# Retention and token/channel mixer on one core: states of three pairs of batch 0 as running sums in PSUM

## The chip, the cores and the metric

The kernel runs on one core of a Trainium2 chip. The core has five engines that run side by side and wait for each other by semaphores: TensorE (PE in the profile; its weight loads are PEld), VectorE (DVE), ScalarE (ACT), GpSimd (POOL) and SyncE (SP). SBUF is the working memory, PSUM (eight banks of 512 f32 columns on 128 partitions) takes what PE writes. The metric is the device time of one execution in microseconds (us), the median of several runs; lower is better.

## The reference

For 4 batches and 8 heads, 768 steps and 64 columns a head, a state decays by a factor `gamma` of its head and takes up an outer product at each step; the query reads it. The result is the input of a mixer over tokens, then one over channels, each with a residual.

```python
gamma = 1.0 - 2.0 ** (-5.0 - np.arange(H))
scale = 1.0 / np.sqrt(D)
for t in range(S):
    state = gamma * state + einsum('bhd,bhe->bhde', k[:, :, t], v[:, :, t])
    y[:, :, t] = scale * einsum('bhd,bhde->bhe', q[:, :, t], state)
x = y.transpose(0, 2, 1, 3).reshape(B, S, H * D)
h = relu(x.transpose(0, 2, 1) @ w_tok1) @ w_tok2
u = x + h.transpose(0, 2, 1)
out = u + relu(u @ w_ch1) @ w_ch2
```

## The kernel before

**Fronts.** For each batch and each pair of heads (4 x 4 fronts) the 768 steps are six chunks of 128. k is scaled by a power of gamma that runs within a chunk (`decayed`, L337; one instruction a head, L343 on ACT or L345 on DVE). k and q are turned by PE (L376, L381), k's turned form is copied out of PSUM (`evkT`, L395), q's is multiplied by a curve of powers on its way out (`qev`, L390). The curves are made once, by exponentials on ACT (L247), of step numbers that GpSimd writes (L235). Within a chunk the scores k x q (`sc`, L457) are masked (`am`, L469) and multiplied with v (`av`, L483). Across chunks, five products k x v (`st`, L410) leave one 64x64 state of each chunk and head in PSUM; U, the running state, is formed on DVE: a copy of the first (L419), then four steps U(c) = g128 U(c-1) + state(c) (L425), where g128 is gamma to the 128th. Two scalings by g128 (`rs`, L435 or L437) put it into block-diagonal tiles `cross` (three of them, tag `rz`), and five products with q add what came from earlier chunks (`y2`, L494). The sum is copied out as x (`xev`, L503). The token mixer follows: `t1` (L520) with w_tok1, relu to h (L529, L531), `t2` (L541) with w_tok2 onto the same bank, u copied out twice (`uev` in f16, `Xev` in f32, both L503), and u turned to `uT` (`tru`, L579, L585; in later batches by DMA).

**Backs.** The channel mixer widens 512 to 1536 columns (`w8`, L617, plain for batch 0's first blocks; P1 to P7, L689, seven products in place of eight) and narrows again (N1 to N7, L787). The seven-product forms need sums: of weights (`asum`, L902; `wsum`, L889), of u (`ts`, L661) and of h (`sm`, L765). X takes up the result (L801) and is stored (L744). The first widening products need uT of pairs 0 to 2 and the first part of w_ch1; wsum needs the whole of w_ch2 (`wc2`, three loads).

**What sets the order.** The program has no scheduler at run time and none that plans at build time: `ORDERED` lists its 1244 operations in the order in which they are issued, `WAYS` says for those with a choice whether ACT or DVE does them, `PLACES` which of the buffers or banks each tile gets, and `FILLS` how many products with zeros PE does ahead of an operation (L921, only in the start-up). Each engine works through its own share in that order, waiting where it must. Loads are issued by GpSimd (L303, L299, and L283 for weights), all on one queue in that order; SP issues the first three (q of pair 0, k of pair 0, q of pair 1), the turnings by DMA and the stores.

Of the kernel before, what the change touches and what calls it, by code (L numbers as in the profile page):

```python
# [10 lines left out]
FP = mybir.dt.float32  # L11
# [5 lines left out]
OPT = dict(wide7=(1, 2, 3), mix=4, turned=(), whole=0, held='qkQ', lead='v00', am=1, turns='twt twt twt twt twt twt twx twx xxx xxx xxx xxx xxx xxx xxx xxx')  # L17
# [10 lines left out]
class Op:  # L28
# [30 lines left out]
    "cW7dd6cPdc707ed71a7fcS726Xdpd86Ydf1c6ZdqcT7gd97hdtcU1jdgdddadr71diduds7idjdedw7jdDdx7kdv8Idn7ldhdEdy",
    "dBdodRdk8LdF7mdzdCdl8adSdAdHdG7ndm7pdTdI8MdV8bdU8N7QdWdK7U7rdYdL7ScD7odXdZ7T1f6v7qdJe07se3dP7Re4e1dM",  # L60
    "dQ7t8d8Je2dN7ueLe98edO7y8fea7ve57A7I8ge69j8OePeM8c7w7ze7eb7JeQe8cE7xed7K8h7B7LeReNee8ief7Mec8K7Neh7O",
    "7PeT8j73eg8Pei8k7W9R7VeUem8Q1e9g8l8R7X7YeSeV7Zen80eOej9h8SeW81bYeqeXek828Tcjes8o8mer83eY8qeZ848p8586",
    "8sf287888neu899O8reAf0ev8Uf39i8WeB9Pey8X9kf18t8V8u8v8w8Zewf4ezci8Y9leC8xf68yexeEel8z9091eF9m8Af79UeD",
    "929Vet938B959W94eH9X969Y9n9S8E8C9ZfaeI8D97f8fb8Ffo8Gfc9o988HeGfefpfgf9ff99fd9pfq9Q9afh9bfsfr9q9c9rfi",
    "ft9T9u9efjfm9wfvfnfk9yfwfQflfC9dg49vfD9ffu9xfAfRfGfxf5fSfBeofHfEg5fya0fTfJ9s9t9zfUfFfzfIfKg6fWfVfLfO",
    "g7fXfPgifY9AfMgjfZ9C9Bg8fNg09D9Egkgmg9g1g2a19Fgng3glgb9GgpeJa2gqgc9Ha69Ka4gugga5gvgoghgAa3gagrhggda7",
    "gshchhge9Jgthi9Ihd9Ma8a9heaahkab9Lachm9NhlgVhngfhohfhqhjhpgRadgThtgWgSgXaehugZgYgwafh0aigUgBh1hrgxgC",
    "gyh3agajgEh2alh4hsgGgzgFh5hvgDakgIh6gHh8gJahgKhxgNh9h7hBgLhahPhyhCi3hbhzhQiheKhFgOhRgMhGhThHhAgPhUhI",
    "hShwhVhJhWiihDhXhKhNilhYhOi1hEhLivgQhMhZi4ijimiJiki2i7ioi0iKinipi5i8i9iqiaitibiNi6iriciLepisifiwidiM",
    "iOizixieiQigiPiAiBiyiCiRjsiDiSiuiViEiHiWiTiIjtj1jJjNjLiFjKjOjTiUjRjoj2jUjPjqjSjXiGjQjVjpjYjyjWjMjwjz",  # L70
    "k0jrjxjZjCiXjAk2iYjujBiZj5k1jDk3j7jEj6jFjvjHj9jGj8j3jIjaj0jbjej4jhjijcjljgjjjdjkjmjfjn00",
)
WAYS = (
    "0000000000000000000000000000000000000000000000000000000000000000000000000000000000000000000010100010",
    "0000000000000000000100100100100000000000000000000000010010000100000000000000000000000000101000001100",
    "0000000000000000000010010000000011000000000001000000000000000000000100000000000000000000000000000000",
    "0001000000000000000000000000100100000100000100000000000000010000000010000010010000000000000000000010",
    "0100100010010000000000000001000001000011000000000010000000000000000000000001100100001000000000000000",
    "0000101101000000000000000000000000000100000010000000000000000000000010000000000000000001000000000100",
    "0000010010001000000010000000000000101000100000000000000000000000000000000000000000000000000000000000",  # L80
    "0000000000000000000000000000000000000000000000000000000000000000000000000000000000011000000000000000",
    "0000000000010000100000000100000000001000000000000000000000000000000000000000000000000000000010000000",
    "0000000000000010000000001000000000100000000000000000000000010000000000000100000001000000000000000000",
    "0000000001000101001000000000000000000000000100000010000000000000110000000000000000000110000000000000",
    "0000000010000000000000001000000010101000000000000010000000001000001001000000000000000000000001110000",
    "00000000000000000000011000000000000010000000",
)
PLACES = (
    "0001101001001021202234506030121131421313054264500356220104250710325040030321403507221110221217311640",
    "7122050662333121702310100571420233504020010216435017025132103012031503016107205231445736501161021745",  # L90
    "2412024211223330200034611012103134061252201112611020741120473534602017533011032201211150212012001765",
    "0324021501640175637303300610710212141127430001221037561124103750302600047316272342045710003511307412",
    "1201601151101233211062701120603012275234476051002751230011220113463173130024571125210303417106430072",
    "2140435244564572011314360702301120230061024017130516413210541102504173601120131",
)
FILLS = (
    (93, 6), (95, 8), (105, 2), (110, 3), (141, 2), (166, 1), (176, 2),
# [18 lines left out]
def kernel(  # L116
# [117 lines left out]
    def emit():  # L234
        nc.gpsimd.iota(tile_of(SINCE, [P, HC, P], FP), pattern=[[0, HC], [1, P]], base=-MID, channel_multiplier=0,  # L235
                       allow_small_or_imprecise_dtypes=True)
    since_op = prep("since", "POOL", 450, emit, takes=[SINCE])
    gq_ops = []
    for p in range(NP):
        def emit(p=p):  # L240
            for j in range(2):
# [3 lines left out]
        def emit(p=p):  # L245
            gq = tile_of(GQ, [P, NP, SH], FP) if GQ.tile is None else GQ.tile
            nc.scalar.activation(gq[:, p], SINCE.tile.rearrange("p i t -> p (i t)"), AF.Exp, bias=lnsc, scale=lnh[:, p:p + 1])  # L247
# [705 lines left out]
```

## Time and profile before

| what | us |
|---|---|
| median of three runs | 186.19 (186.18 to 186.61) |
| the profiled execution | 186.44 |
| its span on the core | 184.7 |
| first to last product of PE | 1.2 to 181.1 |
| TensorE clock granted, mean | 0.999 |

A page of the profile gives each engine's busy time, then the span in 40 slices with the busy share of each in tenths, the DMA queues, and the chain of work that ended last, followed back from the last instruction. A row of the timeline has start, duration, engine, line, operation, tiles written and read with their shapes, and a count where equal ones are merged (the duration then runs from the first start to the last end). Durations of neighbours overlap, so one instruction's cost to its engine is the distance of two starts. A row of the chain has start, the part of time put down to it, engine, tile and line.

These rows are the costliest groups of the start-up on ACT and DVE (0 to 33 us): busy time and mean ns of one, then idle time ahead of them.

```profile
L469 DVE TENSOR_TENSOR am<-psum,mask 128x384 f16<-128x384 f32 x17 | 8.9, 548 | 0.7 <-PE psum L457 0.6
L390 DVE TENSOR_TENSOR qT<-psum,X 128x768 f16<-128x768 f16 x5 | 4.8, 953 | 1.5 <-PE psum L381 1.2 <-PE psum L376 0.2
L425 DVE SCALAR_TENSOR_TENSOR U<-U,gp,psum 128x64 f32<-128x64 f32 x16 | 4.1, 273 | 0.6 <-ACT U L419 0.5
```
```profile
L435 ACT ACTIVATE cross<-U,gp 64x320 f16<-64x320 f32 x8 | 4.5, 556 | 0.1
L343 ACT ACTIVATE k<-k,gk 128x384 f16<-128x384 f16 x5 | 3.0, 613 | 0.7 <-DMA k<-in_k_dram 0.7
```

The eight scalings into `cross` and the sixteen U steps are those of the four pairs of batch 0.

### The profile page before, as it was taken

The numbers are of one execution on the slowest core, as the hardware profiler recorded it, in microseconds if no ns is written. First come the engines' busy times: TensorE is split into PE (matmuls) and PEld (weight loads), VectorE is DVE, ScalarE is ACT, GpSimd is POOL, SyncE is SP. The second block draws the span as 40 slices with busy tenths as digits, with TensorE's granted clock in tenths as the row PEclk, the third lists the DMA queues.
The fourth block names the chain that finished last, engine by engine and source line by source line (L and its number), as shares of the span: only waits on it lengthen the run. The fifth ranks groups of instructions, "written<-read, shape, count | busy, mean of one in ns | idle before, by whom it ended". The sixth has DMA issues, their size and how long they took to land.

```text
span 184.7 us, 5233 instructions
## 1 busy us (share of the span) xinstructions
PE 175.5 (95%) x2054; PEld 133.7 (72%) x2054; DVE 168.7 (91%) x424; ACT 131.5 (71%) x302; POOL 52.2 (28%) x61
## 2 busy tenths in 40 slices
PE   7877989999999999999999999999999999999992
PEld 2445878666688988786568988966678986667881
DVE  5599889999999999999999999989888989889993
ACT  3659989869889997899999778679835324855120
POOL 7985656485282201099020200000000000000000
PEclk9999999999999999999999999999999999999999
DMA  6999999999999999799999895446011034410054
GB/s 158 197 163 184 176 194 207 185 182 194 178 156 158 149 147 131 162 129 139 156 149 227 163 198 132 115 91 166 32 57 31 15 99 171 175 57 0 4 187 155
DMA packets 93993, 25.71 MB, mean 139 GB/s; under 512 B 83600, under 2 KB 91152, under 8 KB 93968
## 3 DMA queue, kind: packets, MB, share of 16 engines
q0 software_dynamic: 67184, 12.78, 85.0%
q1 hardware_dynamic: 25056, 9.83, 25.7%
q10 hardware_dynamic: 1728, 2.75, 4.3%
q8 instruction: 16, 0.26, 0.6%
q14 instruction: 9, 0.07, 0.1%
HBM read 26.74 MB, written 6.29 MB: 179 GB/s over the span
## 4 chain that ended last, share of the span: by engine, by line
PE 71%; DVE 19%; ACT 4%; DMA 2%; issue 2%; DVEq 0%; ACTq 0%
PE psum L689 24%; PE psum L787 23%; PE psum L617 6%; DVE am L469 5%; PE psum L541 4%; PE psum L520 3%; DVE X L801 3%; PE psum L457 3%; DVE U L425 2%; DMA hs<-in_q_dram 2%; DVE hs L765 2%; PE psum L483 2%; PE psum L381 1%; PE psum L376 1%; DVE k L345 1%
## 5 line engine op out<-in xcount | busy, mean ns | idle before, releaser
L642 ACT COPY us<-psum 128x384 f32<-128x384 f32 (+1 forms) x52 | 22.2, 433 | 20.1 <-PE psum L787 13.9
L469 DVE TENSOR_TENSOR am<-psum,mask 128x384 f16<-128x384 f32 x64 | 32.6, 548 | 1.3 <-PE psum L457 1.0
L787 PEld LDWEIGHTS <-hs 128*128 128x128 f16 x282 | 26.6, 98 | 3.7 <-issue 0.4
L303 POOL DMA_DIRECT2D v<-in_v_dram x16 | 16.6, 1036 | 36.9 <-PE psum L494 11.3
L689 PE MATMUL psum<-hs,late 128*128 128x384 f16 x120 | 26.5, 326 | 0.2 <-ACT h L529 0.2
L637 ACT ACTIVATE h<-psum 128x384 f16<-128x384 f32 x47 | 21.8, 492 | 4.4 <-PE psum L617 2.3
L710 DVE CUSTOM_DVE_ANT_0 h<-psum,us 128x384 f16<-128x384 f32 x40 | 21.3, 549 | 1.9 <-ACT us L642 1.3
L787 PEld LDWEIGHTS <-h 128*128 128x128 f16 x216 | 20.6, 98 | 3.1
L689 PEld LDWEIGHTS <-late 128*128 128x128 f16 x160 | 14.9, 98 | 9.3 <-issue 0.4
L801 DVE TENSOR_TENSOR X<-X,psum 128x256 f32<-128x256 f32 (+1 forms) x49 | 19.4, 407 | 1.4 <-PE psum L787 0.7
L787 PE MATMUL psum<-wsum,hs 128*128 128x256 f16 x144 | 19.3, 273 | 0.0
L787 PE MATMUL psum<-wc,h 128*128 128x256 f16 x144 | 19.3, 273 | 0.0
L787 PE MATMUL psum<-wc,hs 128*128 128x256 f16 x138 | 18.7, 273 | 0.0
L303 POOL DMA_DIRECT2D k<-in_k_dram x15 | 15.4, 1030 | 8.6 <-ACT k L343 2.8
L689 PE MATMUL psum<-uT,wc 128*128 128x384 f16 x80 | 17.6, 326 | 0.0
L642 ACT COPY psum<-psum 128x384 f32<-128x384 f32 (+1 forms) x30 | 12.8, 432 | 6.6 <-PE psum L787 3.4
L425 DVE SCALAR_TENSOR_TENSOR U<-U,gp,psum 128x64 f32<-128x64 f32 x64 | 16.3, 273 | 0.9 <-ACT U L419 0.5
L435 ACT ACTIVATE cross<-U,gp 64x320 f16<-64x320 f32 x27 | 15.0, 557 | 1.6 <-DVE U L425 1.1
L689 PEld LDWEIGHTS <-wc 128*128 128x128 f16 x120 | 11.1, 98 | 6.2 <-issue 0.2
L541 PE MATMUL psum<-h,wt 128*128 128x128 f16 x192 | 14.7, 219 | 0.0
L503 ACT CAST x<-psum 128x384 f16<-128x384 f32 x28 | 13.2, 481 | 1.7 <-PE psum L494 0.9
L520 PE MATMUL psum<-x,wt 128*128 128x128 f16 x192 | 13.3, 219 | 0.8 <-ACT X L503 0.6
(90 smaller groups left out, 341.6 us busy)
## 6 DMA issues: line engine op xcount, KB each, us to landing
v<-in_v_dram POOLq DMA_DIRECT2D x16, 192.0 KB, 8.4
out_dram<-X SPq DMA_DIRECT2D x12, 256.0 KB, 2.5
k<-in_k_dram POOLq DMA_DIRECT2D x15, 192.0 KB, 8.3
q<-in_q_dram POOLq DMA_DIRECT2D x14, 192.0 KB, 9.9
wc<-in_moe_w_ch_dram POOLq DMA_DIRECT2D x5, 512.0 KB, 11.5
out_dram<-X ACTq DMA_DIRECT2D x10, 256.0 KB, 2.8
hs<-in_q_dram SPq DMA_DIRECT2D x2, 384.0 KB, 5.0
wc<-in_moe_w_ch_dram POOLq DMA_DIRECT2D x2, 256.0 KB, 9.6
```

The source lines that it names most:

```text
L303: (nc.sync if hard else nc.gpsimd).dma_start(out=tile_of(s, [P, 2, NC, D], FP if hard else F16), in_=src.rearrange("h (c p) d -> p (h c) d ...
L425: nc.vector.scalar_tensor_tensor(out=u[:, c], in0=u[:, c - 1], scalar=gp[:, p:p + 1], in1=chunk(c), op0=ALU.mult, op1=ALU.add)
L435: nc.scalar.activation(r, u, AF.Copy, scale=g)
L469: nc.vector.tensor_tensor(am, SC[g].tile[:, :SH].rearrange("p (i t) -> p i t", t=P), mask.to_broadcast([P, HC, P]), ALU.mult)
L520: nc.tensor.matmul(acc[:, jt * P:(jt + 1) * P], wt1[:, i, jt * P:(jt + 1) * P], X16.tile[:, i].rearrange("p h d -> p (h d)"), start=(i == ...
L541: nc.tensor.matmul(Y[j].tile[:, 2 * i * D:2 * (i + 1) * D], wt2[:, jt, t], H1.tile[:, jt], start=False, stop=(jt == NJ - 1), skip_group_ch ...
L637: nc.scalar.activation(out, src, AF.Relu)
L642: (nc.scalar.copy if e == "ACT" else nc.vector.tensor_copy)(out, src)
L689: nc.tensor.matmul(acc[:, :SH], left(ct), r[:, ct], start=first and ct == 0, stop=ct == C2 - 1, skip_group_check=True)
L710: nc.vector._custom_dve(TENSOR_ADD_SAT, out=h(m, sh), in0=R.tile[:, :SH], in1=KS.tile[:, j], s0=BIG, s1=0.0)
L787: nc.tensor.matmul(acc[:, lo], l[:, j], r[:, j], start=first and j == 0, stop=j == K2 - 1, skip_group_check=True)
L801: nc.vector.tensor_tensor(dst(), dst(), b_(), ALU.add)
```

## The change

For pairs 1, 2 and 3 of batch 0 (`long`), powers of gamma no longer run over one chunk of 128 tokens but over three, 384 tokens, so that chunk states with one scale can be summed by PE in PSUM. k takes its factor from a table `gk2` with three columns (chunk of the half), so each head's scaling is three instructions of 128 columns, each over two chunks. q takes its factor from a second set of curves (three more exponentials on ACT, over a second iota on GpSimd). PE then writes five sums: of chunks 0; 0 and 1; 3; 3 and 4; 0, 1 and 2 (18 products in place of 10). Four evacuations put them into `cross` straight from PSUM: per head a plain copy of the four near sums (`rsn`) and a scaling of the far one by gamma to the 384th (`rsf`). The U copy, the four U steps and the two `rs` of these pairs fall away. The second half's chunks 4 and 5 read two sums each, the near one and the far one, so `y2` has seven products instead of five. Pair 0 of batch 0 and the other batches work as before.

```diff
+        PARTS = ((0,), (0, 1), (3,), (3, 4), (0, 1, 2)) if long else tuple((c,) for c in range(NC - 1))
         def emit():
             st = tile_of(ST, [P, 512], FP)
-            for c in range(NC - 1):
-                for j in range(2):
-                    nc.tensor.matmul(st[rows_of(j), c * D:(c + 1) * D], K.tile[:, c, j], V.tile[:, j, c],
-                                     start=(c == 0), stop=True, skip_group_check=True)
+            for n_, cs in enumerate(PARTS):
+                for c in cs:
+                    for j in range(2):
+                        nc.tensor.matmul(st[rows_of(j), n_ * D:(n_ + 1) * D], K.tile[:, c, j], V.tile[:, j, c],
+                                         start=(n_ == 0), stop=(c == cs[-1]), skip_group_check=True)
...
+        for j, far_ in ((j, x) for j in range(2 if long else 0) for x in range(2)):
+            def emit(e, j=j, far_=far_):
+                cs = slice(NC - 2, NC - 1) if far_ else slice(0, NC - 2)
+                r = opened(RS, None, F16)[rows_of(j), cs, j]
+                u = ST.tile[rows_of(j), cs.start * D:cs.stop * D].rearrange("p (c d) -> p c d", d=D)
+                if e == "ACT" and far_:
+                    nc.scalar.activation(r, u, AF.Copy, scale=g384[rows_of(j), p:p + 1])
+                elif e == "ACT":
+                    nc.scalar.copy(r, u)
...
+            for j in range(2 if long else 0):
+                def emit(e, j=j):
+                    t, h = opened(dst, [P, NC, 2, D], F16)[:, :, j], 2 * p + j
+                    for i in range(HC):
+                        if e == "ACT":
+                            nc.scalar.activation(t[:, i::HC], src.tile[:, j, i::HC], AF.Copy, scale=gk2[:, h, i:i + 1])
...
-            cs = range(max(1, hf * HC), (hf + 1) * HC)
+            cs = [(c, c - 1) for c in range(max(1, hf * HC), (hf + 1) * HC)]
+            if long:
+                cs = [(3, 4), (4, 4), (4, 2), (5, 4), (5, 3)] if hf else [(1, 0), (2, 1)]
...
+            gq2_ops[p] = prep("gq2", "ACT", 620, emit, [since2_op, lnh_op, lgm_op], [], [SINCE, GQ])
...
 FILLS = (
-    (93, 6), (95, 8), (105, 2), (110, 3), (141, 2), (166, 1), (176, 2),
+    (102, 2), (104, 11), (114, 3), (119, 3), (138, 1), (147, 3), (174, 1), (179, 1),
 )
```

The tables `ORDERED`, `WAYS`, `PLACES` and `FILLS` are new throughout: with operations gone and added, the order of all of them, the engine of those with a choice and the banks were chosen afresh. New line numbers stand for old ones thus: L381 and L383 the short decays, L390 and L392 the old ones, L254 and L261 the curves, L443 evkT, L461 st, L488 rs, L499 rsf, L501 rsn, L526 sc, L538 am, L574 the copies of x, u and X, L591 t1, L688 the plain widening, L960 wsum.

Three places of the new order. First ACT, from the scaling of k of pair 1 to the first x, before; `cross` is the block-diagonal state, U the running state, `X_133` the curves, `x` the copies of x.

```order
L343 ACTIVATE k_225<-k_117,gk 128x6x64
L247 ACTIVATE X_133<-us_114,lnsc,lnh 128x384
L395 COPY kT_259<-psum 128x768
L419 COPY U_265<-psum 128x64
L343 ACTIVATE k_283<-k_137,gk 128x6x64 x2
L435 ACTIVATE cross_79<-U_218,gp 64x5x64 x2
L395 COPY kT_325<-psum 128x768
L435 ACTIVATE cross_80<-U_265,gp 64x5x64
L343 ACTIVATE k_337<-k_162,gk 128x6x64
L503 CAST x_359<-psum 128x384
```

The same place of the change, in part: from the turned k of pair 1 to the scaling of k of pair 3.

```order
L443 COPY kT_287<-psum 128x768
L381 ACTIVATE k_291<-k_142,gk_82 128x2x64 x3
L501 CAST cross_79<-psum 64x4x64
L488 ACTIVATE cross_80<-U_233,gp 64x5x64
L499 ACTIVATE cross_79<-psum,g_84 64x64
L443 COPY kT_342<-psum 128x768
L499 ACTIVATE cross_79<-psum,g_84 64x64
L501 CAST cross_79<-psum 64x4x64
L488 ACTIVATE cross_80<-U_233,gp 64x5x64
L501 CAST cross_81<-psum 64x4x64
L499 ACTIVATE cross_81<-psum,g_84 64x64 x2
L381 ACTIVATE k_392<-k_184,gk_82 128x2x64 x6
```

Twelve short decays (three ahead of the first row shown, nine in it) now stand on ACT ahead of the first x, with six evacuations from PSUM; two of the four x copies ahead of t1 are on DVE.

Second DVE, from the second masking of pair 0 to the first of pair 1, before.

```order
L469 TENSOR_TENSOR am_220<-psum,mask 128x384
L425 SCALAR_TENSOR_TENSOR U_218<-U_218,gp,psum 128x64
L469 TENSOR_TENSOR am_223<-psum,mask 128x384
L345 TENSOR_SCALAR k_225<-k_117,gk 128x6x64
L425 SCALAR_TENSOR_TENSOR U_218<-U_218,gp,psum 128x64
L390 TENSOR_TENSOR qT_240<-psum,X_133 128x768
L469 TENSOR_TENSOR am_261<-psum,mask 128x384
```

And in the change, from the third masking of pair 0 on.

```order
L538 TENSOR_TENSOR am_235<-psum,mask 128x384
L383 TENSOR_SCALAR k_237<-k_124,gk_82 128x2x64 x3
L479 SCALAR_TENSOR_TENSOR U_233<-U_233,gp,psum 128x64
L438 TENSOR_TENSOR qT_256<-psum,X_126 128x768
L479 SCALAR_TENSOR_TENSOR U_233<-U_233,gp,psum 128x64 x2
L538 TENSOR_TENSOR am_289<-psum,mask 128x384
L383 TENSOR_SCALAR k_291<-k_142,gk_82 128x2x64 x3
```

Only pair 0 keeps its U steps; the steps of pairs 1 to 3, which stood between the maskings further on, are gone.

Third the loads on GpSimd's queue, ahead of the token mixer's second weights (`wt_83`), before.

```order
L303 DMA k_137<-in_k_dram 128x12x64
L299 DMA q_156<-in_q_dram 128x2x384
L303 DMA k_162<-in_k_dram 128x12x64
L303 DMA v_177<-in_v_dram 128x12x64
L283 DMA wt_82<-in_moe_w_tok_dram 128x6x256
L299 DMA q_216<-in_q_dram 128x2x384
L303 DMA v_237<-in_v_dram 128x12x64
L283 DMA wt_83<-in_moe_w_tok_dram 128x2x384 x2
```

And in the change, where an iota (`since2`) also stands ahead of the second v.

```order
L241 IOTA us_117 128x384
L338 DMA v_132<-in_v_dram 128x12x64
L338 DMA k_142<-in_k_dram 128x12x64
L334 DMA q_163<-in_q_dram 128x2x384
L338 DMA v_168<-in_v_dram 128x12x64
L338 DMA k_184<-in_k_dram 128x12x64
L338 DMA v_207<-in_v_dram 128x12x64
L334 DMA q_231<-in_q_dram 128x2x384
L318 DMA wt_85<-in_moe_w_tok_dram 128x6x256
L318 DMA wt_86<-in_moe_w_tok_dram 128x2x384 x2
```

The first token weights (wt_82, now wt_85) have moved behind v and q of pair 3 (v_237 and q_216, now v_207 and q_231). On PE, one turning of k of batch 1 and the turning of u of pair 3, which stood ahead of the first widening product, now stand behind it; from there to the end PE changes 35 times between half-array and whole-array forms, before 38 times.

More of the change, by code (lines that the diff above doesn't have):

```diff
@@ L414, in chunk @@
         def chunk(c):
             return ST.tile[:, c * D:(c + 1) * D]
-        def emit(e):
-            u = tile_of(US, [P, NC - 1, D], FP)
-            (nc.scalar.copy if e == "ACT" else nc.vector.tensor_copy)(u[:, 0], chunk(0))
-        u0 = op(either(emit, ACT=(110, 214), DVE=(140, 220)), [pp], [US], [ST], key="u0")
-        prev = None
-        for c in range(1, NC - 1):
-            def emit(c=c):
-                u = US.tile
-                nc.vector.scalar_tensor_tensor(out=u[:, c], in0=u[:, c - 1], scalar=gp[:, p:p + 1],
-                                               in1=chunk(c), op0=ALU.mult, op1=ALU.add)
-            prev = op(one("DVE", (195, 280), emit), [pp, gp_ops[p], u0, prev], [], [US, ST], key="u")
@@ new lines, in front, with emit @@
+        if not long:
+            def emit(e):
+                u = tile_of(US, [P, NC - 1, D], FP)
+                (nc.scalar.copy if e == "ACT" else nc.vector.tensor_copy)(u[:, 0], chunk(0))
+            u0 = op(either(emit, ACT=(110, 214), DVE=(140, 220)), [pp], [US], [ST], key="u0")
+            prev = None
+            for c in range(1, NC - 1):
+                def emit(c=c):
+                    u = US.tile
+                    nc.vector.scalar_tensor_tensor(out=u[:, c], in0=u[:, c - 1], scalar=gp[:, p:p + 1],
+                                                   in1=chunk(c), op0=ALU.mult, op1=ALU.add)
+                prev = op(one("DVE", (195, 280), emit), [pp, gp_ops[p], u0, prev], [], [US, ST], key="u")
+            for j in range(2):
+                def emit(e, j=j):
+                    r = (RS.tile if j else tile_of(RS, None, F16))[rows_of(j), :, j]
+                    u, g = US.tile[rows_of(j)], gp[rows_of(j), p:p + 1]
+                    if e == "ACT":
+                        nc.scalar.activation(r, u, AF.Copy, scale=g)
+                    else:
+                        nc.vector.tensor_scalar(r, u, g, None, ALU.mult)
+                rs.append(op(either(emit, ACT=(455 + 115 * j, 555 + 40 * j), DVE=(465, 545)), [u0, prev] + cross_ops, [] if j else [RS],
+                             [RS, US] if j else [US], behind=rs[0] if j else None, key="rs"))
```

166 lines of the change are left out of this document (101 added, 65 removed).

## The prediction

> **What bounds the kernel now.** I read the shares first, then the slices, the chain of waits, and last the first third of the timeline, because the edit sits there.
>
> ```profile
> PE 175.5 (95%) x2054; PEld 133.7 (72%) x2054; DVE 168.7 (91%) x424; ACT 131.5 (71%) x302; POOL 52.2 (28%) x61
> PE   7877989999999999999999999999999999999992
> DVE  5599889999999999999999999989888989889993
> DMA  6999999999999999799999895446011034410054
> PE 71%; DVE 19%; ACT 4%; DMA 2%; issue 2%; DVEq 0%; ACTq 0%
> ```
>
> TensorE (PE) is dense from about the eighth of the 40 slices to the end; only the first seven have holes. VectorE (DVE) is nearly as full up to slice 26, and the DMA engines up to slice 21. The chain, in order of time, gives the border: the first widening product (L617), which ends the start-up, and the last work.
>
> ```profile
> 33.01 0.33 PE psum L617 x2
> ...
> 180.44 0.68 PE psum L835 x12
> ```
>
> So the span of 184.7 is 33.0 us of start-up, 148.1 us of PE without relief and 3.6 us of last adds and stores. Two windows, to both sides of 33.01, say how full each is (PE, PE weight loads, DVE, ACT, POOL, then clock, DMA share, GB/s):
>
> ```profile
> 19.29:33.01 13.72, 12.59 (x235) 11.21 (x236) 12.19 (x29) 12.12 (x27) 8.87 (x11) 1.00 1.54 195
> 33.01:181.15 148.14, 147.83 (x1658) 114.17 (x1656) 140.35 (x334) 106.35 (x252) 28.75 (x29) 1.00 1.08 130
> ```
>
> Behind 33.01 PE idles 0.3 us: nothing is to be had there except PE work itself. Ahead of it DVE and ScalarE (ACT) are both about 89% busy. A gain of this change is therefore a first widening that comes earlier, less what PE then still has to do.
>
> **The parts, VectorE first.** Starts in the timeline stand closer than durations, so I count start to start.
>
> ```profile
> 13.06 0.85 DVE L425 SCALAR_TENSOR_TENSOR U<-U,gp,psum 128x64 f32<-128x64 f32 x4
> 13.83 1.01 DVE L469 TENSOR_TENSOR am<-psum,mask 128x384 f16<-128x384 f32 x2
> 14.76 0.27 DVE L425 SCALAR_TENSOR_TENSOR U<-U,gp,psum 128x64 f32<-128x64 f32 x1
> ```
>
> One U step takes 0.77/4 = 0.19 us, one masking 0.93/2 = 0.47. Twelve steps go: 2.3 us. Ahead of the three uT blocks that open the widening, the new order also takes five evacuations of this size (three u, two uT) from DVE and gives it four (a kT, three of x and X): 0.47 less. One h goes too (256 of 384 columns, 0.3). Four decays become six short ones, which I take as even; at no gain and at the 0.19 of a U step for each short one the bounds are 0 and +1.1. In all DVE has some 3.1 us less there, and is no longer the fuller engine.
>
> **ScalarE takes most of it.** These rows give its prices.
>
> ```profile
> 4.98 1.30 ACT L247 ACTIVATE X<-us,lnsc,lnh 128x384 f32<-128x384 f32 x2
> 8.34 0.83 ACT L356 CAST q<-hs 128x768 f16<-128x768 f32 x1 [1.32 <-DMA hs<-in_q_dram]
> 12.30 0.80 ACT L395 COPY kT<-psum 128x768 f16<-128x768 f16 x1 [1.19 <-PE psum L381]
> 12.99 0.22 ACT L419 COPY U<-psum 128x64 f32<-128x64 f32 x1
> 13.10 1.13 ACT L343 ACTIVATE k<-k,gk 128x384 f16<-128x384 f16 x2
> 14.12 1.12 ACT L435 ACTIVATE cross<-U,gp 64x320 f16<-64x320 f32 x2
> 29.42 0.88 ACT L503 COPY X<-psum 128x384 f32<-128x384 f32 x2
> 30.16 0.84 ACT L395 COPY kT<-psum 128x768 f16<-128x768 f16 x1
> ```
>
> A copy of 64 elements out of PSUM costs 0.11 (12.99 to 13.10), of 384 0.37 ((30.16-29.42)/2), of 768 0.69; so 0.06 and 0.81 ns an element. A decay of 384 out of SBUF costs 0.51 ((14.12-13.10)/2), so its fixed part is 0.20. The decay of 128 elements is not in this trace. Bounds: 0.17, a third of 0.51 (no fixed part), and 0.51 (nothing but fixed part). I take 0.20 + 0.10 = **0.30**, by the two rows for 64 and 384. The near state eviction (256 elements) is 0.27, the far one 0.11.
>
> Now the new ACT order from the landing of the second q (8.34) to the last x of the first two pairs, in its order: cast 0.83, two curves 1.2 (0.6 each, by the 4.98 row: 1.30 for two), three short decays 0.9, two curves 1.2, kT 0.69, three decays 0.9, near 0.27, U 0.56, far 0.11, kT 0.69, far 0.11, near 0.27, U 0.56, near 0.27, two far 0.22, six decays 1.8, near 0.27, curve 0.60, two x 0.74: sum 12.2. So x is complete at 20.5 if ACT never waits. The order has DVE at hand for most feeds; the waits I see (third kT, scores of pair 2 on bank 4) end within 0.2 us of ACT's own time.
>
> *A rule against this.* The Trainium skill, "ScalarE: Activation LUTs", section "Rules for kernel authors", budgets about 0.3 us per ACTIVATE and 0.83 ns an element, which would make a short decay 0.41 us and complete x at 20.5 + 12 x 0.11 = 21.8 (an estimate by that page). The rows above agree on the slope, while two decays started 0.51 apart where that rule gives 0.62.
>
> **The first token product waits for its weights.** On POOL's queue v and q of pair 3 now go ahead of wt1. Issue times, and the times to landing of those issues taken alone:
>
> ```profile
> 8.96 0.85 POOL L283 DMA_DIRECT2D wt<-in_moe_w_tok_dram  x1
> ...
> 11.49 0.75 POOL L283 DMA_DIRECT2D wt<-in_moe_w_tok_dram  x1
> 12.67 0.71 POOL L283 DMA_DIRECT2D wt<-in_moe_w_tok_dram  x1 [0.43 <-DMA k<-in_k_dram]
> ```
> ```profile
> wt<-in_moe_w_tok_dram POOLq DMA_DIRECT2D x1, 384.0 KB, 10.3
> ...
> wt<-in_moe_w_tok_dram POOLq DMA_DIRECT2D x1, 192.0 KB, 10.3
> ...
> wt<-in_moe_w_tok_dram POOLq DMA_DIRECT2D x1, 192.0 KB, 10.1
> ```
>
> wt1 landed at 19.3 (the first window above begins with PE's first t1); the next two landed at 21.8 and 22.8, 1.0 us apart. The queue is backlogged (10 us from issue to landing), so what has landed by a time depends on bytes, not on issue. The set ahead of the second wt is the same in both kernels; wt1 is now its last member, so it lands near 21.8 - 1.0 = 20.8. The extra iota ahead of the second v delays issues by 0.5 us (the existing one is of that length), which the backlog covers; without it the delay would show whole. First t1 then at **20.9**, 1.6 later than before, gated by DMA with 0.4 us of ACT's time to spare. Behind the waiting t1 on PE stand the second t1 and the scores of pair 3; ACT (h, then u) and DVE (maskings of pair 3) run dry meanwhile.
>
> **From there PE itself is the sum.**
>
> ```profile
> 30.15 0.53 PE psum L376 x12
> 30.68 0.44 PE psum L579 x6
> 31.12 0.67 PE psum L541 x12
> 31.79 0.34 PE psum L579 x6
> 32.12 0.44 PE psum L457 x12
> 41.51 0.31 PE psum L410 x20
> 105.34 0.28 PE psum L494 x5
> ```
>
> Between the first t1 and the first widening the new order has four t1 and four t2 (0.67 each, as twelve products of one form: 5.4), two score blocks 0.9, four blocks of six L483 products 0.7 (half of L494's 56 ns for half the width), 14 cross products 0.8, three u transposes 1.0, one k 0.34, one q 0.5: 9.6 us. Changing between half-array and whole-array products shows as 0.10 (the six transposes at 30.68 against those at 31.79); six changes, 0.6. In the old order the same count gives 11.1 us in a stretch of 13.7, thus 2.6 of waits and changes. I allow 1.1, since by the prices above ACT has 8.5 us and DVE 7.0 of work in this stretch, against 12.1 and 12.2 in the old one. First widening at 20.9 + 9.6 + 1.1 = **31.6**, with 33.1 if it waits as before and 31.1 if only for the changes. Against 33.0 that is 1.4 earlier.
>
> **What PE carries over.** One k and one u transpose that stood ahead now stand behind: 2 x 0.34 = 0.7. PE changes form 35 times instead of 38: 0.3 less. The 24 extra state products cost 24 x 0.016 = 0.4 and the six extra cross products 0.3, both ahead of 20.9, where PE waits for weights anyway; if that cover went, they would cost 0.7. The added fill product is there too. The new constants (three curves, two small exponentials, three tiny DVE operations) are in the ACT sum or lie before 8.3, where ACT waited 1.3 us for q. DMA issues on SP move only behind the start. Net: -1.4 + 0.4 = **-1.0 us**. The tail keeps its instructions and its 3.6 us.
>
> The profiled execution took 186.44, 1.76 over its span; 185.4 for its like, and from the median of 186.19: **185.2**.
>
> **Rivals.** *wt1 late, nothing caught up.* t1 is 1.6 us later, and if the stretch behind it keeps 2.6 us of waits, the widening comes at 33.1: +0.1 + 0.4, 186.7; with two thirds of them, 32.2, 185.8. For it: t1, h, t2 and the u copies form one chain over PE, ACT and DVE, however idle these are. Against: DVE falls from 89% to 65%.
>
> *Pinned by c2.* The last block of wc2 was issued at 36.77 and took 13.0:
>
> ```profile
> 36.77 0.74 POOL L283 DMA_DIRECT2D wc<-in_moe_w_ch_dram  x1 [0.37 <-issue]
> 50.68 0.95 DVE L889 TENSOR_TENSOR wsum<-wc 128x1536 f16<-128x1536 f16 x1
> ```
> ```profile
> wc<-in_moe_w_ch_dram POOLq DMA_DIRECT2D x1, 512.0 KB, 13.0
> ```
>
> It landed at 49.8, 0.9 ahead of its use, and the same loads stand ahead of it now. DVE, full there, would wait for it; if PE's order has no room, the gain ends at 0.9 - 0.4 = 0.5: 185.7.
>
> *Slower: short decays at full price.* Twelve of them stand on ACT's chain ahead of t1. At 0.51 each, x completes at 20.5 + 12 x 0.21 = 23.0, the widening at 33.7: +0.7 + 0.4, **187.3**. It decides where ACT passes the weights: at 0.33 each; the gain is gone at 0.42, and at 0.47 the kernel is 0.6 slower. Against it: the 0.11 of the 64-element copy shows that ACT can go on in less than 0.2. By the 0.41 of that page of the Trainium skill the time would be 186.1.
>
> **How the numbers follow.** Measurement tells 0.3% (0.56 us) from no change. The forecast gets 0.52 (0.47 faster, 0.03 same, 0.02 slower, as its 1.1 of waits may be 0.6 or 2); wt1 late 0.20 (0.13 same, 0.07 slower, up to 187.2, since its waits can also exceed the old ones); pinned 0.14 (half faster, half same: 185.7 lies at the limit of 185.6); short decays 0.14 (0.05 same at prices of 0.36 to 0.46, 0.09 slower). Faster 0.54, same 0.28, slower 0.18. The low end is a start-up without waits (31.1: 184.7) and 0.8 that a fuller PE may save behind it, the high end the slower rivals but their last tenth: 183.9 to 187.2.
>
> **What would show it.** The first t1 (now L591) at 20.9 behind a DMA wait; short decays (L381) 0.30 apart on ACT; the first widening (L688) at 31.6; PE from there to its last product 148.5; wsum (L960) not before 49.8. Wrong is the forecast if t1 waits for x and not for wt, if the first L688 is behind 32.5, or if PE behind it idles more than 0.5 us.

## The result, and the profile after

| | before | after |
|---|---|---|
| median, us | 186.61 (186.18 to 186.93, 5 runs) | 191.84 (190.24 to 193.04, 5 runs) |
| profiled execution, its span | 186.44, 184.7 | 190.95, 189.2 |
| first token product (t1) | 19.29 | 22.80 |
| first widening product | 32.84 | 33.20 |
| end of PE's last product | 181.1 | 185.3 |

The change makes the kernel slower: ratio 1.0279, 95% interval 1.0213 to 1.0345. The forecast was 185.2, and its range of 183.9 to 187.2 does not hold the time. The runs also spread over 2.8 us, those before over 0.75. The spread goes with the granted clock: the two runs of the change with a mean of 0.991 took 190.2 and 191.0, the three with 0.982 took 191.8 to 193.0. The medians further on are over all runs of a kernel; one run of cold_fills (193.82) was in a slower state of the chip and is left out of its ratio.

The shares and slices on the page of the changed kernel (engines, then PE's busy tenths and the granted clock, then the chain that ended last):

```profile
PE 178.2 (94%) x2085; PEld 135.4 (72%) x2085; DVE 165.5 (87%) x418; ACT 136.8 (72%) x325; POOL 53.1 (28%) x62
PE   7887799999999999978999999999999999999991
PEclk9999699999999999999999999999999999999999
PE 77%; DMA 5%; ACT 3%; DVE 2%; issue 1%; DVEq 0%
```

DVE was relieved as announced (91% to 87% of a longer span), and the chain no longer runs over DVE (19% to 2%). In its place stands DMA with 5% (before 2%), and PE has 77% (before 71%). PE has two new marks: a clock of 0.6 in the fifth slice, and holes in slices 18 and 19. So there are two places to look at, the start-up and the stretch around 80 us. Two windows of the changed kernel (PE, PE weight loads, DVE, ACT, POOL, then clock, DMA share, GB/s), as the prediction cut them for the kernel before:

```profile
22.80:33.20 10.40, 10.33 (x195) 9.55 (x194) 7.58 (x15) 9.65 (x23) 6.11 (x7) 0.97 1.52 196
33.20:185.33 152.13, 149.40 (x1674) 115.11 (x1670) 141.04 (x332) 109.28 (x263) 28.61 (x30) 1.00 1.09 126
```

From the first widening to the last product PE takes 152.1 where 148.5 was forecast, and idles 2.7 of them. The 4.5 us of longer span are thus 0.4 in the start (33.20 against 32.84 in PE's timeline), 3.9 behind it (152.1 against 148.3 from 32.84 to 181.1) and 0.3 in the tail.

**Around 80 us.** The chain of waits of the changed kernel, in order of time (start, time put down, what):

```profile
73.75 9.06 DMA uT<-u
...
82.89 0.57 DVE hs L732
...
83.50 0.48 PE psum L760 x2
```

A transposition of u by DMA, issued at 73.75, landed 9.06 later; a difference on DVE (L732) and PE's products (L760) waited for it. On PE the wait falls between the two halves of P2, the first product to read these two turned tiles:

```profile
81.49 0.32 PE L760 MATMUL psum<-uT,wc 128*128 128x384 f16 x1
82.85 0.32 PE L760 MATMUL psum<-uT,wc 128*128 128x384 f16 x1 [1.04 <-DMA uT<-u]
```

The other waits of PE from 70 to 95 that the trace lists, 1.6 in all, are for ACT and DVE, which had themselves waited there: DVE 2.5 for the same uT, ACT 0.9 for a turned q. What landing took for the two turnings of u by DMA at this place, by the view of the tile uT, before and after:

```profile
DMA to landing us min/median/max: 2.7/3.6/4.5
```
```profile
DMA to landing us min/median/max: 7.7/8.4/9.1
```

And what SP and GpSimd issue there in the changed kernel:

```profile
69.56 2.21 SPq L411 DMA_TRANSPOSE qT<-q  x1
71.82 3.35 SPq L639 DMA_TRANSPOSE uT<-u  x2
75.28 1.77 SPq L411 DMA_TRANSPOSE kT<-k  x1
```
```profile
69.62 1.01 POOL L338 DMA_DIRECT2D v<-in_v_dram  x1 [6.23 <-PE psum L565]
70.62 2.06 POOL L338 DMA_DIRECT2D k<-in_k_dram  x2
72.67 1.03 POOL L338 DMA_DIRECT2D q<-in_q_dram  x1
```

Three loads of the last batch (two k, one q, 192 KB each) now fall among the transpositions. In the kernel before they stood behind a load of v that waits for its buffer, and GpSimd issued nothing from 69.9 to 78.0:

```profile
78.03 1.02 POOL L303 DMA_DIRECT2D v<-in_v_dram  x1 [8.16 <-DVE am L469]
```

**The start.** PE's timeline of the changed kernel (start, time, line, operation, tiles, count, then idle time ahead and what ended it):

```profile
19.68 1.19 PE L428 MATMUL psum<-ident,k 128*128 128x128 f16 x6 [1.26 <-ACT k L381]
20.67 0.53 PE L552 MATMUL psum<-v,am 128*128 128x64 f16 x6
21.01 0.40 PE L565 MATMUL psum<-cross,qT 128*128 128x128 f16 x2
21.34 0.69 PE L461 MATMUL psum<-v,k 128*64 128x64 f16 x18
21.84 0.83 PE L423 MATMUL psum<-ident,q 128*64 128x128 f16 x12
22.80 0.90 PE L591 MATMUL psum<-x,wt 128*128 128x128 f16 x8
```

PE waits 1.26 for the decayed k of pair 3. The masked and cross products of the first half of pair 1 (L552, L565 at 20.67) stand behind that turning in PE's order, and DVE's copies of x behind these products:

```profile
21.52 0.56 DVE L574 CAST x<-psum 128x384 f16<-128x384 f32 x1 [2.36 <-PE psum L565]
...
22.19 0.56 DVE L574 CAST x<-psum 128x384 f16<-128x384 f32 x1
```

The weights had landed by then: wt1 was issued at 11.5 and took 9.0, so 20.5. The first t1 waited for x. ACT in the same stretch:

```profile
17.71 0.63 ACT L499 ACTIVATE cross<-psum,g 64x64 f16<-64x64 f32 x2
18.35 1.86 ACT L381 ACTIVATE k<-k,gk 128x128 f16<-128x128 f16 x6
20.24 0.37 ACT L501 CAST cross<-psum 64x256 f16<-64x256 f32 x1
20.63 0.71 ACT L254 ACTIVATE X<-us,lnsc,lnh 128x384 f32<-128x384 f32 x1
21.36 0.86 ACT L574 CAST x<-psum 128x384 f16<-128x384 f32 x2
```

The short decays start 0.31 apart (six from 18.35 to 20.24), as forecast; but a far copy of 64 elements (L499, 17.71 to 18.35 for two) costs 0.32, not 0.11, a near one (L501) up to 0.39, not 0.27. And the copy at 20.24 frees the bank into which the products of 20.67 go.

### The profile page after: what moved, and what is told of

It is laid out like the page before. It is cut to its first block, busy times and chain, and to the rows that moved or that the text cites. A ratio compares the mean times of both kernels' runs of the same rounds, so it can differ in the third digit from the quotient of the medians.

```text
span 189.2 us, 5329 instructions
## 1 busy us (share of the span) xinstructions
PE 178.2 (94%) x2085; PEld 135.4 (72%) x2085; DVE 165.5 (87%) x418; ACT 136.8 (72%) x325; POOL 53.1 (28%) x62
## 4 chain that ended last, share of the span: by engine, by line
PE 77%; DMA 5%; ACT 3%; DVE 2%; issue 1%; DVEq 0%
PE psum L858 27%; PE psum L760 25%; PE psum L688 5%; PE psum L591 5%; DMA uT<-u 5%; PE psum L612 5%; PE psum L552 2%; PE psum L526 2%; PE psum L565 2%; PE psum L461 1%; PE psum L428 1%; PE psum L650 1%; PE psum L423 1%; ACT u L574 1%; DVE x L574 1%
## 5 line engine op out<-in xcount | busy, mean ns | idle before, releaser
L713 ACT COPY us<-psum 128x384 f32<-128x384 f32 (+1 forms) x55 | 23.9, 439 | 17.2 <-PE psum L858 8.5
L538 DVE TENSOR_TENSOR am<-psum,mask 128x384 f16<-128x384 f32 x64 | 32.1, 548 | 2.8 <-ACT h L600 1.6
L760 PE MATMUL psum<-hs,late 128*128 128x384 f16 x120 | 25.6, 326 | 0.9 <-ACT psum L713 0.5
L708 ACT ACTIVATE h<-psum 128x384 f16<-128x384 f32 x45 | 21.3, 499 | 4.6 <-PE psum L760 3.8
L760 PEld LDWEIGHTS <-late 128*128 128x128 f16 x160 | 14.9, 98 | 11.8 <-issue 2.8
L760 PE MATMUL psum<-uT,wc 128*128 128x384 f16 x80 | 18.5, 326 | 1.4 <-DMA uT<-u 1.0
L760 PEld LDWEIGHTS <-wc 128*128 128x128 f16 x120 | 11.1, 98 | 7.0 <-issue 1.0
L574 ACT CAST x<-psum 128x384 f16<-128x384 f32 x27 | 12.2, 485 | 4.5 <-PE psum L565 4.3
L574 ACT CAST u<-psum 128x384 f16<-128x384 f32 x27 | 12.7, 488 | 3.6 <-PE psum L612 3.2
L591 PE MATMUL psum<-x,wt 128*128 128x128 f16 x192 | 13.5, 222 | 0.1
L479 DVE SCALAR_TENSOR_TENSOR U<-U,gp,psum 128x64 f32<-128x64 f32 x52 | 13.1, 274 | 0.2
```

Source lines behind the costliest of these rows:

```text
L479: nc.vector.scalar_tensor_tensor(out=u[:, c], in0=u[:, c - 1], scalar=gp[:, p:p + 1], in1=chunk(c), op0=ALU.mult, op1=ALU.add)
L538: nc.vector.tensor_tensor(am, SC[g].tile[:, :SH].rearrange("p (i t) -> p i t", t=P), mask.to_broadcast([P, HC, P]), ALU.mult)
L574: (nc.scalar.copy if e == "ACT" else nc.vector.tensor_copy)(tile(), t)
L591: nc.tensor.matmul(acc[:, jt * P:(jt + 1) * P], wt1[:, i, jt * P:(jt + 1) * P], X16.tile[:, i].rearrange("p h d -> p (h d)"), start=(i == ...
L708: nc.scalar.activation(out, src, AF.Relu)
L713: (nc.scalar.copy if e == "ACT" else nc.vector.tensor_copy)(out, src)
```

## The experiments

All edits but cold_fills move operations, by a list `MOVES` of pairs (n, m) that is read behind `ORDERED`: operation n is put directly behind operation m, with its buffer or bank. x_first and the three runs that contain all its moves also give one operation to another engine; cold_fills only adds products of zeros. The list and its reading shift the line numbers of these runs by 7 to 9.

```diff
+    for n, m in MOVES:
+        seq.remove(ops[n])
+        seq.insert(seq.index(ops[m]) + 1, ops[n])
```

| run | first t1 | first widening | last product | median, us | ratio to before |
|---|---|---|---|---|---|
| the change | 22.80 | 33.20 | 185.3 | 191.84 | 1.0279 (1.0213 to 1.0345) |
| loads_late | 22.99 | 34.20 | 186.1 | 191.84 | 1.0293 (1.0260 to 1.0326) |
| loads_dec_late | 22.76 | 33.22 | 182.4 | 188.31 | 1.0104 (1.0077 to 1.0132) |
| before_loads_early | 19.33 | 32.69 | 181.6 | 187.28 | 1.0054 (1.0038 to 1.0070) |
| cold_fills | 22.59 | 32.89 | 187.3 | 191.83 | 1.0275 (1.0213 to 1.0336) |
| x_pe_only | 21.77 | 32.70 | 185.5 | 190.16 | 1.0197 (1.0146 to 1.0249) |
| x_first | 20.80 | 31.68 | 182.6 | 188.98 | 1.0147 (1.0122 to 1.0171) |
| x_first_loads_dec | 20.73 | 31.65 | 180.6 | 186.44 | 0.9995 (0.9975 to 1.0016) |
| two_waits_less | 20.68 | 31.61 | 180.8 | 186.85 | 1.0047 (1.0030 to 1.0064) |
| decays_behind_copies | 21.22 | 32.14 | 181.3 | 186.59 | 1.0018 (1.0005 to 1.0031) |

The three middle columns are those of one profiled execution; two of them with the same start differ there (loads_late moves nothing ahead of 70 us, and its first widening is 1.0 later than that of the change; the mean clock up to 33 us is 0.95 in both, but the 3.4 us at half clock lie at 22.5 to 25.9 in loads_late and at 20.0 to 23.4 in the change). Medians are compared through the kernel before, which ran beside each.

### The loads: loads_late, loads_dec_late, before_loads_early

loads_late sets k of pair 0, k of pair 1 and q of pair 0 (79, 82, 81) behind the waiting load of v (80).

```diff
+MOVES = (
+    (79, 80), (82, 79), (81, 82),
+)
```

> The changed kernel, with three loads of the last batch (k and q of pair 0, k of pair 1), which it issued at 70.6, 71.7 and 72.7, set behind the load of v of pair 0, which waits for its buffer until 78.7; nothing else moves. Theory A (loads among the DMA transposes make them slow): the transposes issued from 69.6 to 77.2, which took 7.1 to 10.7, take 1.5 to 5 as before the change, TensorE's gaps between 75 and 93 fall from about 4.9 to about 1.5, and the time falls by 3 to 4, from 191.8 to about 188. Theory B (six transposes one behind the other fill the queue by themselves): the transposes stay at 7 or more and the time within 0.6 of 191.8. Theory C (most of the loss is the colder and later start): as B.

The transpositions behaved as theory A has it: those of u took 5.1 and 3.3 instead of 7.7 and 9.1, the next k 3.5 instead of 9.4, the next q 4.5 instead of 10.6. The time did not move. Busy times from 72 to 92, first for the kernel before, then for the change, then for loads_late:

```profile
72.00:92.00 20.00, 19.98 (x226) 14.32 (x225) 19.52 (x46) 18.61 (x44) 10.08 (x10) 1.00 1.84 149
```
```profile
72.00:92.00 20.00, 17.34 (x204) 12.81 (x202) 16.14 (x41) 15.06 (x37) 7.75 (x8) 1.00 1.73 149
```
```profile
72.00:92.00 20.00, 16.93 (x210) 13.20 (x208) 15.64 (x44) 15.29 (x39) 9.09 (x9) 1.00 1.63 134
```

PE lost 2.7 of the 20 in the change and 3.1 in loads_late. ACT's timeline of loads_late shows what came in place of the old wait:

```profile
84.61 0.39 ACT L607 ACTIVATE h<-psum 128x256 f16<-128x256 f32 x1
88.13 0.61 ACT L397 ACTIVATE k<-k,gk 128x384 f16<-128x384 f16 x1 [3.13 <-DMA k<-in_k_dram]
```

The order has a decay of the last batch on ACT at this place, and it now waited 3.13 for a load that landed late; the copies that PE waits for stood behind it. The order had been laid out around the early load. So the run shows what the loads do to the transpositions and decides nothing on the time. The next one moves two decays of the last batch too: 506 on ACT behind 822, a copy that stands 51 places further on in the order (13 operations of ACT), next to its second head, and 540 on DVE behind 826.

```diff
+MOVES = (
+    (79, 80), (82, 79), (81, 82), (506, 822), (540, 826),
+)
```

> loads_late once more, and with it the first decay of k of pair 0 of the last batch on ScalarE, which waited 3.1 at 85.0 for the load that now lands at 88.1 with TensorE's copies queued behind it, set behind 26 later operations (next to its second head), and the first decay of k of pair 1 on VectorE likewise. Theory A (the loads among the transposes cost the time, and loads_late only moved the wait to the decay that stood ready for the early load): TensorE's gaps between 75 and 93 fall from 4.9 to 1.5 or less, and the time falls by 2.5 to 4, from 191.8 to 188 or 189.3. Theory B (the changed order is too dense there in any case: ScalarE and VectorE, not the transposes): another wait comes in their place, gaps stay at 3.5 or more, and the time is within 1 of 191.8.

The time fell to 188.31, 3.5 less than the change (3.4 through the kernel before). The turnings of u took 4.7 and 3.2, and PE is full:

```profile
72.00:92.00 20.00, 19.86 (x233) 14.67 (x232) 18.70 (x48) 17.89 (x43) 9.09 (x9) 1.00 1.73 147
```

In the change PE was busy 17.34 there, so 2.5 us come back in this window alone; a little is left, as the kernel before has 19.98. Theory B falls: the same transpositions follow each other just as closely, on the same order of work but for two decays. No run moves these decays alone; in the change the one on ACT runs at 86.65, takes 0.5 and waits for nothing, and of PE's listed waits there only one, of 0.4, lies behind it.

The reverse, on the kernel before: k of pairs 1 and 3 and q of pair 1 (73, 78, 75) behind the load of v that is issued at 68.7 (71), ahead of the one that waits.

```diff
+MOVES = (
+    (73, 71), (78, 73), (75, 78),
+)
```

> The kernel before, with three loads of the last batch (k of pairs 1 and 3, q of pair 1), which it issued from 79.0 on behind a load of v that waits for its buffer until 78.0, set ahead of that load: they are then issued at about 70, 71 and 72, among its DMA transposes of u, q and k. Theory A: the transposes issued from 69.5 to 77.1, which took 2.7 to 5.5, take 7 or more, TensorE waits for uT or kT, and the time rises by 2 to 4, from 186.5 to 188.5 or 190.5. Theory B: the transposes keep their times, and the time is the same within 0.6.

The transpositions became slower nearly as expected: the loads were issued at 69.7, 70.7 and 71.7, and the transpositions issued from 69.4 to 77.3 took 6.1 to 7.5, where 7 or more was expected. The two turnings of u, by the view of uT:

```profile
DMA to landing us min/median/max: 6.7/6.8/6.9
```

The time rose by 1.0 (0.38% to 0.70%), less than the 2 to 4 expected: PE waits neither for uT nor for kT, and its busy time from 72 to 92 falls only from 19.98 to 19.68. The two turnings are those of pairs 2 and 3 of u, which P2 reads; P1, ahead of it, reads pairs 0 and 1, which PE turns. In the kernel before, P2 starts at 79.61, 4.0 behind the second landing (75.6). Here that landing came 3.9 later, at 79.5, and P2 started at 79.46: the room was just used up. The changed order has no less room: in loads_dec_late the second turning lands at 77.0 and P2 starts at 80.82. But in the change this turning took 9.1 where it took 3.2 in loads_dec_late, 5.9 longer, and PE waited. A transposition that takes longer costs what goes beyond the slack of its consumer. Why the same number of loads delayed it more in the changed order, no run separates.

What the contention is made of was not tried. The Trainium skill, "DMA: Bandwidth & Descriptors", section "SWDGE vs HWDGE vs iDMA", says that transfers issued by GpSimd and by SP run on the same 16 engines, each of which takes turns between their queues. The runs agree as far as they go: three loads more in the stretch, and a transposition takes 6.1 to 10.7 us instead of 2.7 to 6.2.

### The start: cold_fills, x_first, x_pe_only

The clock falls behind PE's wait. Two windows of the changed kernel (last columns: clock, DMA share, GB/s), the second of them the whole of the fall:

```profile
16.62:20.03 3.41, 1.70 (x30) 1.31 (x29) 1.95 (x4) 3.32 (x11) 2.51 (x3) 1.00 1.42 197
20.04:23.44 3.40, 3.24 (x50) 2.73 (x51) 1.87 (x5) 3.30 (x8) 1.88 (x3) 0.50 1.73 182
```

cold_fills tests what that costs, by products of zeros that cover the wait.

```diff
 FILLS = (
-    (102, 2), (104, 11), (114, 3), (119, 3), (138, 1), (147, 3), (174, 1), (179, 1),
+    (202, 5), (102, 2), (104, 11), (114, 3), (119, 3), (138, 1), (147, 3), (174, 1), (179, 1),
```

> The changed kernel, with five products of zeros (0.216 each) added on TensorE ahead of the turn of k of pair 3, where it waits 1.26 from 18.42. They add no work that anything waits for, unless they end behind 19.68 (5 x 0.216 = 1.08 ends at 19.5). Theory (the wait itself let the clock fall, which then cost about 1.0 in products that ran at half speed from 19.7 to 24): the clock is full from 18 to 25, the turn takes 0.5 instead of 1.2, the first L591 is at 21.8 to 22.3 and the first widening at 32.2 to 32.6 instead of 33.2. Rival (the clock is no cause; VectorE and ScalarE set the first L591): it stays at 22.6 to 22.9 and the first widening at 33.0 to 33.3. The whole time falls by at most 1 in either, as the loads stay as they are.

```profile
18.36 1.24 PE L992 MATMUL psum<-zero 128*128 128x512 f16 x5
19.78 0.98 PE L428 MATMUL psum<-ident,k 128*128 128x128 f16 x6 [0.18 <-ACT k L381]
...
22.59 0.61 PE L591 MATMUL psum<-x,wt 128*128 128x128 f16 x8 [0.65 <-DVE x L574]
```

The clock stayed at 1.00 from 15 to 25, yet the first t1 came only 0.2 earlier and the widening 0.3, and the turn took 0.98 at full clock too, where the expectation had 0.5: with PE faster, x was still late. The rival holds for t1 (22.59; the widening, at 32.89, lies just below its 33.0), and in the start the clock is an effect of the wait more than a cause of the loss. The whole time did not change within its spread; in this execution PE waited 2.5 for uT at 81.3, and from 85.6 to 89.0 the clock was at 0.50.

x_first takes the order itself: PE's products of pair 1 (152 and 154 stand together, 202 is the turning) go ahead of the turning, the copy that frees their bank (177) ahead of the decays on ACT, the second head of these decays (201) to DVE, where it waited 0.64, and a curve (12) behind ACT's copies of x.

```diff
+MOVES = (
+    (177, 178), (201, 151), (202, 154), (12, 157),
+)
...
+    for n, w in ((201, '1'),):
+        ways = ways[:n] + w + ways[n + 1:]
```

> The changed kernel, with the masked and cross products of the first half of pair 1 ahead of the turn of k of pair 3 on TensorE, the copy of pair 2's states that frees their bank ahead of pair 3's decays on ScalarE, the second head of these decays on VectorE where it waited 0.6, and a curve for pair 1 of the next batch behind the copies of x. The loads stay. Theory C (the start lost its gain because x of pairs 0 and 1 stands behind the turn that waits for six short decays, and TensorE cooled while it waited): x is complete at about 20.5 instead of 22.7, the first product of token mixing (L591) at 20.6 to 21.2 instead of 22.80, behind the DMA of its weights or behind TensorE's own work, the granted clock in the 5 us around 20 is not below 0.95, and the first widening is at 31.4 to 32.0 instead of 33.2; the time falls by 1 to 1.8 if what stands behind follows. Rival (the start is bound elsewhere, as by ScalarE's sum of work): the first L591 is still behind 22, the widening behind 32.8, and the time is within 0.6.

```profile
18.66 0.33 PE L561 MATMUL psum<-v,am 128*128 128x64 f16 x6 [0.23 <-ACT cross L510]
18.83 0.28 PE L574 MATMUL psum<-cross,qT 128*128 128x128 f16 x2
19.09 0.98 PE L437 MATMUL psum<-ident,k 128*128 128x128 f16 x6
20.00 0.47 PE L470 MATMUL psum<-v,k 128*64 128x64 f16 x18
20.31 0.51 PE L432 MATMUL psum<-ident,q 128*64 128x128 f16 x12
20.80 0.84 PE L600 MATMUL psum<-x,wt 128*128 128x128 f16 x12
```

First t1 at 20.80, first widening at 31.68, clock 1.00: theory C, and the forecast's own two numbers (20.9 and 31.6). wt1 landed at 20.8 here and ACT's last copy of x ended at 20.5, but with three decays and a curve less ahead of it. The time fell by 2.9 (2.5 through the kernel before), more than the 1.5 of the start and the 1 to 1.8 expected. PE's busy time from 72 to 92 is 18.2 here against 17.3, so the wait for the transpositions, which is still there, was shorter in this execution; why, no run separates.

x_pe_only keeps only the first and the third move.

```diff
+MOVES = (
+    (177, 178), (202, 154),
+)
```

> x_first without two of its four moves: VectorE keeps none of pair 3's decays (all six stay on ScalarE) and the curve for the next batch stays ahead of ScalarE's copies of x; what is left are the products of pair 1 ahead of the turn of k of pair 3, and the copy that frees their bank ahead of the decays. If the place of these products behind the waiting turn was the cause, VectorE's copies of x are done by 20.2 instead of 22.7, and only ScalarE's two (behind six decays and a curve of 0.7) hold x back, to about 21.8: first L591 at 21.8 to 22.0, first widening 32.2 to 32.7, 1 less than the changed kernel. If the load on ScalarE was the cause, the first L591 stays behind 22.5 and the widening behind 32.9.

First t1 at 21.77, the widening at 32.70. The 2.0 us that x_first gains at t1 are thus half PE's order (22.80 to 21.77) and half ACT's load (21.77 to 20.80).

### Both, and what is left: x_first_loads_dec, two_waits_less, decays_behind_copies

> x_first and loads_dec_late together. If the start and the loads are the whole loss: first widening at 31.4 to 32.0 as in x_first, gaps between 72 and 91 at 1.5 or less, and a time of 185.0 to 186.0, against 186.24 before: the forecast's value for the change. If loads and start are not independent, or another wait comes behind 75: 187.5 to 189.

The edit is the sum of those of x_first and loads_dec_late. 186.44, ratio 0.9995: undoing both places takes back the whole loss of 5.2 us, and the change is then worth nothing that can be measured. Singly they gave 2.5 and 3.4 through the kernel before, 0.6 more than together; x_first by itself already lost 0.9 less of PE's time from 72 to 92. The start came as expected, and PE is busy 19.7 of 20 from 72 to 92; the time is 0.4 above the expectation. Its windows:

```profile
20.73:31.65 10.92, 10.37 (x198) 9.34 (x195) 7.66 (x15) 10.44 (x25) 6.63 (x8) 1.00 1.59 193
31.65:180.59 148.94, 148.58 (x1674) 114.81 (x1670) 140.13 (x332) 109.06 (x263) 29.52 (x30) 1.00 1.15 131
```

1.2 earlier at the widening (31.65 against 32.84), 0.7 more behind it (148.94 against 148.27): 0.5 at the last product, of which 0.2 goes in the tail (3.8 against 3.6).

The last two runs look for more. In the trace of x_first_loads_dec PE's successive starts leave 0.30 open at 81.35 and 0.34 at 89.83. two_waits_less moves what stands ahead there on ACT: 399 (a copy of X) behind 804 (a seed, L722), 506 and 507 (decays) and 508 (their transposition) behind the copy 825. The seed then writes its bank before the copy of X has read it, so one block of X gets other values; the amount of work stays.

```diff
+MOVES = (
+    (79, 80), (82, 79), (81, 82), (506, 822), (540, 826), (177, 178), (201, 151), (202, 154), (12, 157), (399, 804), (506, 825), (507, 506), (508, 507),
+)
```

> x_first_loads_dec, with its two longest waits of TensorE behind 75 (0.30 at 81.35 and 0.34 at 89.83) taken on: a copy of X on ScalarE, which waits 0.48 for VectorE, set behind the copy (L722's seed) that TensorE waits for at 81.8; the two decays of k of pair 0 (88.07 to 89.2) and the transpose that they feed set behind the copy that TensorE waits for at 90.3. If these waits set the end, as the order of TensorE is one chain from there on: 0.4 to 0.6 less than x_first_loads_dec, 185.8 to 186.0, which is 0.5 under the kernel before. If slack behind them takes it up, or the delayed copy and transpose are waited for in their turn: 186.2 to 186.6, no gain.

```profile
PE psum L769 <- ACT us L722: 0.8, 1, 0.8
```

Of PE's waits behind 33 us this is now the only one in the list: the wait at 81 is gone, that at 90 has grown from 0.34 to 0.94, since the decays stand ahead of the next copy instead. 186.85, no gain. decays_behind_copies leaves 399 and 804 alone, puts the decays behind all four copies (behind 860), and 787 (a difference of u) behind 398 on DVE.

```diff
+MOVES = (
+    (79, 80), (82, 79), (81, 82), (506, 860), (507, 506), (508, 507), (540, 826), (177, 178), (201, 151), (202, 154), (12, 157), (787, 398),
+)
```

> x_first_loads_dec with the two decays of k of pair 0 of the last batch, and their transpose, behind all four copies on ScalarE that TensorE waits for between 87 and 91.5 (in two_waits_less they stood between the first and the second, and the wait grew from 0.34 to 0.94 there), and with VectorE's copy of u, for which ScalarE waits 0.48 at 80.3, ahead of a difference of u that is used later. Nothing else of two_waits_less. If these two waits (0.30 at 81.35, 0.34 at 89.83) are paid in full: 185.8 to 186.1 and gaps of TensorE between 80 and 92 of 0.9 or less. If one of them only moves: 186.2 to 186.6, as x_first_loads_dec.

The wait at 90 is gone and that at 81 has 0.23 left (PE is busy 19.9 of 20 from 72 to 92), but 0.8 of gaps came at 92.5 to 93.4, ahead of and within a block of scores (L535). From the first widening to the last product it is 149.1 against 148.9, and 186.59 is no gain. (Its start, with the same moves, came 0.5 later in this execution; why, no run shows.) No order tried beats the kernel before.

## Why the prediction was wrong

- **Short decays on ACT, 0.30:** right (0.31). The rival that priced them higher was right on the sign only. The rule of the Trainium skill that was weighed there ("ScalarE: Activation LUTs", "Rules for kernel authors") gave 0.41: one decay lasts 0.39 in the trace, but back to back they start 0.29 to 0.31 apart.
- **ACT's sum, x complete at 20.5:** failed, its part was done at 22.2. ACT hardly idled (13.5 of 13.9 us busy from 8.3 to 22.2); the term that was too small is the copies out of the state bank, of which eight stand ahead of the first x: the sum had all eight, the text on the order counts six. Four far ones at 0.32 instead of 0.11 are 0.8, four near ones at 0.26 to 0.39 instead of 0.27 another 0.3, and the rest is 0.1 each on the start, the second kT, a curve and the copies of x. The 0.11 is the price of a plain copy to U, and it holds for that: in the change too, eight plain ones of 64 elements let the next instruction start 0.09 to 0.14 later. The far copies are another instruction, with a scale, over 64 partitions and into f16, and all six of them took 0.31 to 0.33; which of the three makes the price, no run separates. The sum took the price of the one for the other.
- **First t1 at 20.9, gated by wt1 with 0.4 of slack on ACT:** failed. wt1 landed at 20.5, the forecast's 20.8 was near, but x was complete only at 22.75, on DVE. The sum of ACT alone left out that x also needs products on PE, which stood in PE's queue behind a turning that waits for ACT's last decays, and in a bank that a copy behind these decays frees. x_pe_only and x_first show it: each half of the cure brings 1.0, and the full one the forecast's 20.8 to 20.9. That it came out there does not bear out ACT's sum, since x_first takes three decays and a curve, some 1.5, from ACT ahead of x.
- **From t1 to the widening 9.6 + 1.1 = 10.7:** right. 10.4 in the change, 10.9 in x_first; in the change PE idled 0.1 of it. The rival "wt1 late, nothing caught up" is out.
- **Extra products hidden ahead of 20.9:** PE had 1.26 of wait there, room for their 0.7; no run tested it by itself.
- **PE from widening to last product 148.5, nothing to be had or lost behind 33:** failed, 152.1, and this is the greater part of the loss: 3.9 of the 4.5 in the profiled executions. The step that failed is the sentence that DMA issues on SP move only behind the start, with nothing put down for it, and GpSimd's loads not looked at past the start. The order moved three loads 8.4 us forward, among the transpositions; loads_dec_late gives 3.5 us back by moving them away, and with them the decays that had been laid out for them. It is then 148.9 to 149.1, 0.7 to 0.9 above the 148.3 of the kernel before, where 0.4 was put down for carried-over PE work; PE's busy time alone is 0.6 to 0.8 above.
- **Pinned by wc2:** out. The first wsum (now L960) starts at 52.3, 2.4 behind the landing of wc2 at 49.9.
- **The direction:** the range was built from the start alone, with all its rivals there. None could give more than 187.3.

## What to carry to other kernels

An order that is searched anew moves every queue, also where the edit changes nothing; compare the issue times of loads and of transpositions by DMA over the whole span before summing the edit, since a load moved into a burst of transpositions cost each of them up to 6 us here, and whoever consumes them pays what goes beyond the slack. When a tile is complete is the latest of the queues it passes: an engine's own sum says little if a product it needs stands behind another engine's wait. And a load moved back takes its consumers' place in their queues along, or the wait only changes its engine.

## What the runs showed of the hardware

- A transposition by DMA that was issued at 66 to 77 us took 2.7 to 6.2 us where GpSimd issued one load between 67 and 76 us, and 6.1 to 10.7, from about the first load on, where it issued four (in both orders).
- The clock stood at half (0.50) for 3.4 us, 20.0 to 23.4 in the change, although PE's longest wait was 1.26: in the 3.4 us ahead PE had been busy 1.7. The same fall follows 2.0 busy of 3.4 in loads_late and 1.4 of 3.4 in cold_fills (85.6 to 89.0, behind the wait for uT). The Trainium skill, "TensorE: Matmul & The Clock Gate", section "What's actually happening", ties the lower clock to an idle window of about 3.4 us; here a half-used stretch was enough, and five products of zeros (2.7 busy of 3.4) kept the clock at 1.00. One such fall is 0.009 of the mean clock over 189 us (an estimate: half of 3.4 over 189), so the runs of the change at 0.982 would have had two, where its trace, at 0.991, shows one.
- A copy of 64 elements out of PSUM with a scale took ACT 0.31 to 0.33 from start to start, a plain one 0.09 to 0.14 where the next instruction was ready.
